# Nyström attention and a feed-forward layer on one core: batches 1 to 7 move to batch 0's tile layout, and the DMA crossbar turns q and k

## The chip, the cores and the metric

The kernel runs on one core of a Trainium2 chip, in one launch. The metric is device time in microseconds. The kernel before takes 267.89 us in the median of three runs (267.88, 267.89, 268.66).

## The reference

Eight batches, eight heads, 576 tokens, head size 64; 32 landmarks, each the mean of 18 consecutive tokens. Cut to what is computed:

```
q_lm, k_lm = means of q and k over segments of 18 tokens      # 32 landmarks
A = softmax(q k_lm^T / 8);  Bm = softmax(q_lm k_lm^T / 8);  C = softmax(q_lm k^T / 8)
Z = Bm^T / (norm1(Bm) * norminf(Bm))
six times:  Z = 2 Z - Z Bm Z
x   = A Z C v                     # heads side by side: (8, 576, 512)
xn  = (x - mean(x)) / sqrt(var(x) + 1e-6) * g_ln
out = x + relu(xn W1) W2          # W1: 512 x 2048, W2: 2048 x 512
```

Inputs and output are fp32; the kernel computes its products in fp16 with fp32 sums.

## The kernel before

**Units and stages.** A unit is four heads of one batch, so a batch has two units (u = 0, 1). For each unit q, k and v are loaded as 576 KB tiles `stg` (128 partitions: a head pair times 64 token groups; nine tokens in the row of each), cast to fp16 (`nat` for q and k, `natv` for v), q and k are turned so that the head dimension lies on the partitions (`xT`), and landmark sums are formed. Then follow the k scores, the exponentials, their product with v (`pscv`), the iteration on 32x32 blocks (`st`), the q scores (`ea`), and their divisors (`psd`, `lns`). The attention is not written out and read again: the 32x64 heads matrix Z C v is turned (`pszt`, `zt`), multiplied into W1 (`bank<-w,zt` or `psm`, copied to `m`), and the first layer takes `m` and `ea` directly (`psh`, then ReLU into `hT`). The rows of x themselves (`xblk`) are formed once, for the mean, the variance and the residual (`bank<-zcbd,ea`, `six`, `stats`, `rstd`). The second layer is `bank<-w,hT`; batches 4 to 7 do 512 of their 576 rows with seven half-size products in place of eight (`w2mix`).

**Batch 0** (`attention0`) is turned by TensorE against an identity (`pst`), each 128x128 block at once. Its landmark sums are nine 128x64 matmuls against `pm16`; q's landmarks are masked per head into `qbd`, so that `psc` multiplies full 128-row columns of `xT` by `qbd`, 18 matmuls a unit, and the result is exponentiated straight into the layout that `pscv` needs (`ect`). The q scores `psa` take 64-row pieces.

**Batches 1 to 7** (`Coming`, `attention2`, in the sets (1), (2), (3, 4), (5, 6), (7)) are turned by VectorE as 32x32 blocks of fp16 pairs seen as uint32 (`StreamTranspose xT<-nat`). That leaves rows of 32 partitions, so the scores are 32x32 tiles of TensorE with 288 columns, in two accumulated halves (`psec`, `psea`); the k scores are exponentiated by three ScalarE steps a unit (`ec`) and turned once more by VectorE (`ecT`). Landmark sums come in three ways: nine 128x128 matmuls against `pairs16` and a small turn (`tot`, `lmt`; batch 1 and half of set (3, 4)), VectorE sums over `xT` (`part<-xT`), or four adds on GpSimd (`asum`, `s`); `spread16` then distributes them (two matmuls a pair of units, `lm`).

**W1** holds g_ln and has its column means taken off so that the layer norm's mean drops out. `less(f)` is the mean of a quarter of W1. Up to batch `LAST_WHOLE` = 1 the copies of `m` add that term (`SCALAR_TENSOR_TENSOR m<-less,zsum,bank`); after it `center_w1` subtracts it from W1 itself in eight VectorE steps (`w<-w,less`), and `m` is a plain copy on whichever of ScalarE and VectorE is free sooner (`sooner`).

**What sets the order.** The program is written at build time by a planner. `Clock` keeps an estimated time for each engine and tile. Five streams (0 attentions, 1 totals, 2 first layers, 3 rows of batch 0, 4 second layers) yield when their next step can start, and the first stream in that list that can go now does:

```
            at = [when(k) for k in range(len(streams))]
            k = next((k for k in range(5) if at[k] <= now), None)
```

Between steps `help_out` issues stores, loads, casts, VectorE jobs, measuring and centring when the clock says that the engine is about free. The table `AFTER` holds a given step back until another stream has come so far (33 entries before). All engines run their own instructions strictly in the order written. All loads and stores but a few at the end go through SyncE's queue; SBUF buffers are rings (`stage` 6, `nat` 6, `xT` 4 for q and 4 for k), and PSUM has two two-bank tiles (`ps2`) and four single banks.

The helper `keep` (line 248) records every instruction; so most rows of the profile have line 298 (VectorE, ScalarE, GpSimd), 304 (`MM`), 308 (`TR`), 313, 321 and 323 (loads; the latter two load the second unit of v in three pieces, `load_swapped`), 434 and 451 (W1 and W2) or 1216 (stores), and are told apart by their tiles.

Of the kernel before, what the change touches and what calls it, by code (L numbers as in the profile page):

```python
# [20 lines left out]
def kernel(  # L21
# [63 lines left out]
    class Clock:  # L85


        WAY = 55.0
        OVERLAP = {"Activation": 110, "DVE": 80, "Pool": 30}
# [41 lines left out]
        def took(self, i, e, n, m):  # L131
            op = type(i).__name__
            if e == "Activation":
                return 300 if n < 8 else 190 + (1.07 if name_of(i.outs[0].bass_ap).startswith("ec_") else 0.79) * n
# [22 lines left out]
        def note(self, i):  # L157
# [33 lines left out]
            elif e == "PE":  # L191
                cols = count[0]
                if self.count == self.mark - self.LEAD:
                    self.ahead = self.now()
                if self.count == self.mark:
                    self.mark += self.BLOCK
                    ready = max(ready, self.fetched)
                    asked = max(self.ahead, self.fetched - 200)
                    behind = max([w for t, w in self.loads if t <= asked] + [0.0])
                    self.fetched = max(asked + 1200, behind + 400) + 2450  # L200
                self.count += 1
                rows_, cols_ = tuple(i.tile_size)
                self.cells.append((self.now(), cols / 2.4 * rows_ * cols_ / 128 ** 2))
                if tuple(i.tile_size) == (128, 128):
                    if self.small:
                        self.free[e] = max(list(self.lanes.values()) + [self.free[e]]) + 100
                        self.small, self.lanes = False, {}
                    start = max(self.free[e], ready)
                    self.free[e] = start + max(cols / (1.2 if start < 5200 else 2.4) + 3, 56)
                    done = self.free[e] + 160  # L210
                else:
                    if not self.small:
                        self.small, self.lanes = True, {}
                        self.free[e] += 95
                    elif self.shape != (rows_, cols_):
                        self.free[e] = max(list(self.lanes.values()) + [self.free[e]]) + 85
                    self.shape = rows_, cols_
                    lane = [(a, c) for a in range(i.tile_position[0], i.tile_position[0] + rows_, 32)
                            for c in range(i.tile_position[1], i.tile_position[1] + cols_, 32)]
                    start = max([self.free[e], ready] + [self.lanes.get(x, 0.0) for x in lane])  # L220
                    self.lanes.update((x, start + max(cols / 2.4, 30)) for x in lane)
                    self.free[e] = start + (8 if rows_ == 64 and cols < 128 else 4)
                    done = self.lanes[lane[0]] + 160
            else:
                start = max(self.free[e], ready)
                self.ready = start
                done = start + self.took(i, e, count[0], max(count[1:] + [0]))
                self.free[e] = done - self.OVERLAP[e]
                if e == "Pool":
                    self.pool = self.pool[-8:] + [(start, done)]  # L230
                if e == 'DVE' and count[0] == 1024 and writes[0] in parted_w1:
                    self.free['Pool'] = max(self.free['Pool'], start) + 430
            for n in reads:
# [69 lines left out]
    def MM(o, l, r, rb=0, cb=0, start=True, stop=True, skip=False):  # L303
        keep(nc.tensor.matmul(o, l, r, start=start, stop=stop, tile_position=(rb, cb),  # L304
                              skip_group_check=(skip or cb != 0)))

    def TR(o, i_, idn):
        keep(nc.tensor.matmul(o, i_, idn, is_transpose=True, tile_position=(0, 0)))


    def load(src, b, u, queue, t=None):
# [4 lines left out]
        return t  # L316

    def load_swapped(src, b, u, queue):
        t = stage.tile([P, 2, NJ, D], FP32, name="stg", tag="stg")
        heads = src[b, 4 * u:4 * u + 4].rearrange("h (t j) d -> h t j d", j=NJ)  # L320
        keep(queue.dma_start(out=t[:, 0, :, :], in_=heads[1:3].rearrange("h t j d -> (h t) j d")))
        for e in range(2):
            keep(queue.dma_start(out=t[ts(1 - e, 64), 1, :, :], in_=heads[3 * e]))
# [10 lines left out]
    for u in range(U):  # L334
# [19 lines left out]
    pairs16 = const.tile([P, 2, 2, LM], FP16, name="pairs16")  # L354
    nc.gpsimd.tensor_copy(
        out=pairs16[:], in_=pm16[:].rearrange("p (e l) -> p e l", e=2)[:, :, None, :]
        .broadcast_to([P, 2, 2, LM]))

# [12 lines left out]

    heads4 = const.tile([P, 2, 2, 2], FP32, name="heads4")
    for x in range(2):
        for e in range(2):
            nc.gpsimd.tensor_copy(out=heads4[:, x, :, e], in_=mask4[:, ts(e ^ x, 2)])
    heads_of = [heads4[:, x, :, :].rearrange("p r e -> p (r e)") for x in range(2)]
    spread16 = const.tile([P, 2, 2, 2, LM], FP16, name="spread16")
    nc.gpsimd.memset(spread16[:], 0.0)
    for half in range(2):
        for e in range(2):  # L380
            sl = ds(64 * e + 32 * half, 32)
            nc.gpsimd.tensor_copy(
                out=spread16[sl, half, e, :, :],
                in_=ident16[sl, sl][:, None, :].broadcast_to([LM, 2, LM]))
# [174 lines left out]

    heads, ready, multiplied, cast_v = {}, set(), {0}, {0}  # L560
# [8 lines left out]
    def attention0():  # L569
# [5 lines left out]
        def p2(shape, dtype, name):  # L575
            return ps2.tile(shape, dtype, name=name, tag="p2")

        qbd = asm.tile([P, W * 2, 2, LM], FP16, name="qbd", tag="qbd", bufs=1)
        dve.tensor_tensor(
            out=qbd[:],  # L580
            in0=nat_pss[0][:].rearrange("p u (e l) -> p (u e) l", e=2)[:, :, None, :]
            .broadcast_to([P, W * 2, 2, LM]),
            in1=mask2[:, None, :, None].broadcast_to([P, W * 2, 2, LM]), op=ALU.mult)
        yield "q's landmarks"
        klm = asm.tile([P, W, 64], FP16, name="klm", tag="klm", bufs=1)
# [6 lines left out]
        for w in range(W):  # L592
            for h in range(4):
                e, r = h // 2 ^ w, h % 2
                MM(psb[ds(32 * h, 32), w, :], qbd[ds(64 * r, 64), 2 * w + e, r, :],
                   klm[ds(64 * r, 64), w, ds(32 * e, 32)], rb=64 * r, cb=32 * h)
# [5 lines left out]
        for w in range(W):  # L602
            psc = p2([P, NJ, 64], FP32, "psc")
            for j in range(NJ):
                for e in range(2):
                    MM(psc[ds(64 * e, 64), j, :], early_xT["k", w][:, j, ds(64 * e, 64)],
                       qbd[:, 2 * w + e, :, :], cb=64 * e)
            t = aexp.tile([P, NJ, 64], FP16, name="ect", tag="e")
            act(t[:], psc[:], AF.Exp, scale=sc_C)
            ect.append(t)  # L610
# [17 lines left out]
        def scores_of_q(w):  # L628
            psa = p2([P, NJ, 64], FP32, "psa")
            for (j0, j1) in ((0, 8), (8, NJ)):  # L630
                for h in range(4):
                    r, e = divmod(h, 2)
                    rows, cb = ds(64 * r, 64), 32 * (2 * (e ^ w) + r)
                    MM(psa[ds(cb, 32), j0:j1, :], klm[rows, w, ds(32 * e, 32)],
                       early_xT["q", w][rows, j0:j1, ds(64 * e, 64)], rb=64 * r, cb=cb)
            t = aexp.tile([P, NJ * 64], FP16, name="ea", tag="e")
            act(t[:], psa[:].rearrange("p j t -> p (j t)"), AF.Exp, scale=sc_A)
            ea.append(t[:])

        warm(4, 256)  # L640
# [4 lines left out]

        def cv_of(w, h, half=None):
            at, n = ((D + 1) * (h % 2), D) if half is None else ((D + 1) * (h % 2) + 32 * half, 32)
            return cv[ds(32 * h, 32), w, ds(at, n)]
# [26 lines left out]
        zt = asm.tile([P, 2, W, LM], FP16, name="zt", tag="zt")  # L675
        for w in range(W):
            pszt = p2([P, 2, 512], FP32, "pszt")
            for h in range(4):
                e, r = h // 2 ^ w, h % 2
                sl = ds(32 * h, 32)  # L680
                for half in range(2):
                    cb = 64 * e + 32 * half
                    MM(pszt[ds(cb, 32), r, 0:LM], cv_of(w, h, half), st[sl, w, LM:],
                       rb=32 * h, cb=cb)
            scalar.copy(zt[:, :, w, :], pszt[:, :, 0:LM])
# [3 lines left out]
        for w in range(W):  # L689
            for h in range(4):  # L690
                sl = ds(32 * h, 32)
                MM(pszc[sl, w, :], st[sl, w, LM:], cv_of(w, h), rb=32 * h, cb=32 * h)
# [83 lines left out]
    class Coming:  # L776
        def __init__(self, bs, by_dve, by_pe=()):
# [7 lines left out]
            self.jobs = []  # L785
            for i, (nm, w) in enumerate(self.parts[:2 * n]):
                self.jobs.append((self.turn, i))
# [1010 lines left out]
```

## Time and profile before

| | before |
|---|---|
| median of three runs | 267.89 us (267.88 to 268.66) |
| span of the profiled execution | 266.1 us |
| the profiled execution's own time | not recorded apart; the median is 1.8 us above the span |
| granted TensorE clock, mean | 0.999 |
| instructions | 8332 |
| DMA | 46.68 MB, of it 36.70 MB read from HBM and 9.44 MB written |

The page gives busy time by engine, then forty slices of 6.65 us each in tenths, DMA queues, the chain of waits that ended last, and the costliest groups. A matmul's duration in a row includes its way through the array; matmuls overlap, so the distance between starts is less than the duration (a 128x512 `bank<-w,hT` has 380 ns in its row). "Idle before" is the engine's idle time ahead of the group, with what ended it.

### The profile page before, as it was taken

To read this page: it belongs to the slowest core of one execution; us is meant where nothing else is said; L and a number is where in the kernel's file an instruction comes from. 1 tells how busy PE (TensorE), PEld (TensorE's weight loads), DVE (VectorE), ACT (ScalarE), POOL (GpSimd) and SP (SyncE) were. 2 spreads that over 40 slices of the span, in tenths; PEclk is the share of its full clock that TensorE was granted. 3 is DMA by queue.
4 is the path that set the end of the run, shared out by engine and by line. 5 is a ranking of instruction groups with operands and counts; after the bars stand their busy time and mean duration, and the time that the engine had idled before them with its cause. 6 is when DMAs were issued, how large, how long until landed. Compare 5 with 4: busy or idle time off the path is not lost.

```text
span 266.1 us, 8332 instructions
## 1 busy us (share of the span) xinstructions
PE 256.5 (96%) x3442; PEld 167.9 (63%) x3442; DVE 202.8 (76%) x461; ACT 175.2 (66%) x337; POOL 133.6 (50%) x160
## 2 busy tenths in 40 slices
PE   7889998999999999999999999999999999999994
PEld 7644754466545554546655465578878765788883
DVE  2657873899999979788984986989684599819762
ACT  2578997378868896589797559787377654871000
POOL 5288788999729387499999934500000042000000
PEclk9999999999999999999999999999999999999999
DMA  7999999999976996766611120110060006100606
GB/s 253 380 396 389 388 386 393 317 343 306 354 237 172 388 363 187 207 174 198 200 43 39 34 52 2 42 43 0 2 158 0 2 4 160 43 0 2 158 17 183
DMA packets 23566, 46.68 MB, mean 175 GB/s; under 512 B 2404, under 2 KB 2664, under 8 KB 23528
## 3 DMA queue, kind: packets, MB, share of 16 engines
q1 hardware_dynamic: 23048, 45.49, 53.3%
q10 hardware_dynamic: 480, 0.66, 0.7%
q8 instruction: 27, 0.44, 0.7%
q14 instruction: 11, 0.09, 0.1%
HBM read 36.70 MB, written 9.44 MB: 173 GB/s over the span
## 4 chain that ended last, share of the span: by engine, by line
PE 78%; DMA 11%; DVE 3%; POOL 3%; issue 2%; SPq 1%; ACT 1%; POOLq 0%; DVEq 0%
PE bank L304 51%; PE psh L304 21%; DMA stg<-in_v_dram 6%; DMA wstg<-in_moe_w_ch_dram 3%; DMA stg<-in_q_dram 2%; PE pscv L304 1%; POOL natv L298 1%; PE psd L304 1%; DVE xblk L298 1%; PE psec L304 1%; PE psm L304 1%; PE psea L304 1%; POOL w L298 1%; SPq L313 1%; DVE st L298 1%
## 5 line engine op out<-in xcount | busy, mean ns | idle before, releaser
L304 PE MATMUL bank<-w,hT 128*128 128x512 f16 (+3 forms) x528 | 111.7, 335 | 1.2 <-issue 0.8
L298 ACT ACTIVATE hT<-psh 128x576 f16<-128x576 f32 x119 | 73.6, 654 | 21.9 <-PE psh L304 21.0
L304 PEld LDWEIGHTS <-hT 128*128 128x128 f16 x656 | 60.3, 98 | 32.5 <-issue 8.6
L304 PE MATMUL psh<-ea,m 128*128 128x288 f16 x512 | 78.3, 286 | 0.6 <-DVE ea L298 0.3
L304 PEld LDWEIGHTS <-m 128*128 128x128 f16 x512 | 48.8, 97 | 20.2 <-issue 3.7
L298 DVE SCALAR_TENSOR_TENSOR xblk<-bank,rstd,xblk 128x256 f32<-128x256 f32 (+2 forms) x77 | 39.0, 539 | 22.4 <-PE bank L304 22.3
L298 POOL TENSOR_TENSOR ea<-ea,lns 128x576 f16<-128x576 f16 x14 | 18.9, 1371 | 60.4 <-ACT lns L298 54.6
L298 POOL CAST nat<-stg 128x1152 f16<-128x1152 f32 x21 | 23.8, 1147 | 8.5 <-DVE xT L298 6.4
L298 DVE BATCH_NORM_STATS2 six<-xblk 128x6 f32<-128x512 f32 x36 | 24.2, 673 | 0.9 <-ACT xblk L298 0.9
L298 POOL CAST natv<-stg 128x1152 f16<-128x1152 f32 (+1 forms) x17 | 19.3, 1165 | 9.7 <-DMA stg<-in_v_dram 7.7
L298 DVE STREAM_TRANSPOSE xT<-nat 128x576 uint32<-128x576 uint32 x28 | 21.4, 763 | 0.0
L298 ACT COPY xblk<-bank 128x512 f32<-128x512 f32 (+1 forms) x32 | 18.0, 591 | 4.0 <-PE bank L304 3.7
L304 PE MATMUL bank<-w2mix 128*128 128x256 f16 x128 | 17.1, 273 | 0.0
L304 PE MATMUL bank<-w2mix,hT 128*128 128x256 f16 x128 | 15.8, 273 | 0.0
L298 DVE SCALAR_TENSOR_TENSOR st<-st,bank 128x128 f16<-128x128 f16 (+2 forms) x36 | 11.1, 308 | 5.9 <-PE bank L304 5.7
L298 ACT CAST m<-bank 128x512 f16<-128x512 f32 x18 | 9.9, 586 | 7.5 <-PE bank L304 7.4
L298 DVE TENSOR_REDUCE part<-xT 128x32 f16<-128x576 f16 x20 | 14.6, 744 | 0.2
L298 ACT ACTIVATE lns<-psd 128x576 f32<-128x576 f32 x16 | 10.3, 644 | 6.0 <-PE psd L304 5.9
L304 PE MATMUL bank<-zcbd,ea 128*128 128x256 f16 x80 | 14.1, 273 | 0.0
L298 DVE SCALAR_TENSOR_TENSOR m<-less,zsum,bank 128x512 f16<-128x512 f16 (+1 forms) x18 | 11.5, 682 | 3.0 <-PE bank L304 1.4
L304 PEld LDWEIGHTS <-w2mix 128*128 128x128 f16 x128 | 12.4, 98 | 2.0 <-issue 0.2
L304 PEld LDWEIGHTS <-st 32*32 32x32 f16 x448 | 5.9, 90 | 11.9 <-DVE st L298 8.9
(135 smaller groups left out, 365.9 us busy)
## 6 DMA issues: line engine op xcount, KB each, us to landing
stg<-in_q_dram SPq DMA_DIRECT2D x16, 576.0 KB, 6.3
stg<-in_k_dram SPq DMA_DIRECT2D x16, 576.0 KB, 6.0
out_dram<-xblk SPq DMA_DIRECT2D x66, 128.0 KB, 2.4
wstg<-in_moe_w_ch_dram SPq DMA_DIRECT2D x16, 512.0 KB, 7.3
stg<-in_v_dram SPq DMA_DIRECT2D x10, 576.0 KB, 7.2
stg<-in_v_dram SPq DMA_DIRECT2D x6, 288.0 KB, 6.2
stg<-in_v_dram SPq DMA_DIRECT2D x12, 144.0 KB, 6.0
out_dram<-xblk ACTq DMA_DIRECT2D x4, 128.0 KB, 3.2
```

Source lines behind the costliest of these rows:

```text
L298: return lambda *args, **kw: keep(getattr(self.engine, op)(*args, **kw))
L304: keep(nc.tensor.matmul(o, l, r, start=start, stop=stop, tile_position=(rb, cb), skip_group_check=(skip or cb != 0)))
L313: keep(queue.dma_start(out=t[:], in_=src[b, 4 * u:4 * u + 4].rearrange("(r e) (t j) d -> (e t) r j d", e=2, j=NJ)))
```

## The change

- Sets (1) to (7) use batch 0's layout: `nat` is [128, 9, 128], `xT` is a full turn [128, 9, 128], and k scores, exponentials, products and q scores are the same code for all batches (`scores_of_landmarks`, `scores_k`, `scores_q`, `masked_q`, `heads_to_rows`).
- q and k of batches 2 to 7 are turned by a DMA transpose on SyncE's queue, SBUF to SBUF, 24 in all; those of batch 1 by TensorE, as batch 0's. VectorE turns none.
- Landmark sums: batch 1 by TensorE (`pm16`, nine matmuls a tile); k of batches 2 to 7 by one VectorE sum over `xT`; q of batches 2 to 7 by GpSimd's four adds and one 128x64 matmul.
- `pairs16`, `spread16`, `lm`, `lmt`, `ec`, `ecT` and `load_swapped` go; v of all units is one load and one cast.
- `LAST_WHOLE` is 0: W1 is centred after batch 0's products, and batch 1's `m` are plain copies.
- The planner prices a DMA transpose (`TURN_ISSUE`, `TURN_WIRE`), takes a second-layer step in place of a first-layer step when an attention step is due within 400 ns (`SOON`), lets second-layer steps wait for W2's casts, and has a new `AFTER` table of 15 entries. `attention0` has four more filler matmuls.

The diff, cut to its core:

```diff
+        TURN_ISSUE, TURN_WIRE = 700.0, 1000.0
...
+            elif type(i).__name__ == "InstDmaTransposeAnt":
+                start = max(self.free[e], ready)
+                self.free[e] = start + self.TURN_ISSUE
+                self.wire = max(start + 1650, self.wire) + self.TURN_WIRE
+                self.loads = self.loads[-24:] + [(start, self.wire)]
+                done = start = self.wire + 600
...
+    def masked_q(lm):
+        t = asm.tile([P, 2 * U, 2, LM], FP16, name="qbd", tag="qbd", bufs=3)
+        dve.tensor_tensor(out=t[:], in0=lm..., in1=mask2x..., op=ALU.mult)
+        return t
+
+    def scores_k(x, qbd, xT):
+        psc = ps2.tile([P, NJ, 64], FP32, name="psc", tag="p2")
+        for j in range(NJ):
+            for e in range(2):
+                MM(psc[ds(64 * e, 64), j, :], xT[:, j, ds(64 * e, 64)],
+                   qbd[:, 2 * x + e, :, :].rearrange("p r l -> p (r l)"), cb=64 * e)
+        t = aexp.tile([P, NJ, 64], FP16, name="ect", tag="e")
+        act(t[:], psc[:], AF.Exp, scale=sc_C)
+        return t
+
+    def scores_q(pair, klm, xT):
+        tiles = {x: ps2.tile([P, NJ, 64], FP32, name="psa", tag="p2") for x in pair}
+        for (j0, j1) in ((0, 8), (8, NJ)):
+            for e in range(2):
+                for r in range(2):
+                    for x in pair:
+                        rows, cb = ds(64 * r, 64), 32 * (2 * (e ^ x) + (r ^ x))
+                        MM(tiles[x][ds(cb, 32), j0:j1, :], klm[rows, x, ds(32 * e, 32)],
+                           xT[x][rows, j0:j1, ds(64 * e, 64)], rb=64 * r, cb=cb, skip=True)
...
         def turn(self, i):
             nm, w = self.parts[i]
-            t = aprep.pin(aprep.tile([P, 2, NJ, LM, 2], FP16, name="xT", tag="xT" + nm, bufs=4))
-            n16 = self.n16[i]
-            dve.transpose(t[:].rearrange("p r j t x -> p (r j t x)").bitcast(UINT32),
-                          n16[:].rearrange("p r j d -> p (r j d)").bitcast(UINT32))
+            t = aprep.pin(aprep.tile([P, NJ, P], FP16, name="xT", tag="xT" + nm, bufs=4))
+            keep(nc.sync.dma_start_transpose(
+                out=t[:], in_=self.n16[i][:].rearrange("p j r d -> p (j r d)")))
             self.used(i)
...
+        def add_up(self, i):
+            ...
+                dve.tensor_reduce(
+                    out=self.lm[nm, w // 2][:, w % 2, :],
+                    in_=self.xT[nm, w][:].rearrange("p j (g a) -> p g j a", a=2),
+                    axis=AX.XY, op=ALU.add)
...
-    LAST_WHOLE = 1
+    LAST_WHOLE = 0
...
-    sets = [Coming((1,), (), ("k0", "k1", "q0", "q1"))]
+    sets = [Coming((1,), (), ("k0", "q0"))]
+    sets += [Coming(bs, [f"k{y}" for y in range(len(bs))]) for bs in ((2,), (3, 4), (5, 6), (7,))]
...
+                if c.turns:
+                    if c.turn_ready() <= now and clock.free["SP"] <= now + 500:
+                        c.next_turn()
...
+            if k == 2 and at[0] <= now + SOON and at[4] <= now:
+                k = 4
```

In the changed program TensorE has 3211 matmuls in place of 3442; VectorE 326 instructions in place of 383, ScalarE 175 in place of 210, GpSimd 112 in place of 104. SyncE's queue holds 24 transposes more and 12 split v loads less.

More of the change, by code (lines that the diff above doesn't have):

```diff
@@ L190, in note @@
                 start = done
[L191 to L223, printed above, removed]
@@ L592, in attention0 @@
         for w in range(W):
[L593 to L596, printed above, removed]
+            scores_of_landmarks(psb, w, qbd, klm, w)
         act(psb[:], psb[:], AF.Exp, scale=sc_B)
@@ L602, in attention0 @@
         for w in range(W):
[L603 to L610, printed above, removed]
+            ect.append(scores_k(w, qbd, early_xT["k", w]))
         cinv, _ = gram_of(p1([P, 4, W * LM], "psse"), st, bmT, W, lambda: warm(2, 256))
@@ L628, in scores_of_q @@
         def scores_of_q(w):
[L629 to L638, printed above, removed]
+            ea.extend(scores_q((w,), klm, {w: early_xT["q", w]}))
+        warm(4, 256)
         warm(4, 256)
@@ L833, in used, with turn_ready, job_ready @@
                 nat.unpin(self.n16.pop(i))
[L835 removed]
+        def turn_ready(self):
+            i = self.turns[0]
             if i not in self.n16:
                 return NEVER
[L838 to L842 removed]
+            return max(clock.at(self.n16[i]), aprep.next("xT" + self.parts[i][0]))
+        def job_ready(self):
+            i = self.jobs[0]
+            return clock.at(self.xT[self.parts[i]]) if self.parts[i] in self.xT else NEVER
@@ new lines, in lm_next, with add_ready, add @@
+        def lm_next(self, i):
+            nm, w = self.parts[i]
+            return asm.next("klm" if nm == "k" else "qbd")
+        def add_ready(self, i):
+            of = self.sums if self.how(i) == "pool" else self.n16
+            if i not in of or i + 1 not in of:
+                return NEVER
+            return max(clock.at(of[i], of[i + 1]), banks.next(), self.lm_next(i))
+        def add(self, i):
+            psl = banks.take([P, U, 64])
+            for x in range(U):
+                if self.how(i) == "pool":
+                    s16 = self.sums.pop(i + x)
+                    asm.unpin(s16)
+                    MM(psl[:, x, :], s16[:].rearrange("p r d -> p (r d)"), pm16[:], skip=True)
+                else:
+                    for j in range(NJ):
+                        MM(psl[:, x, :], self.n16[i + x][:, j, :, :].rearrange("p r d -> p (r d)"),
+                           pm16[:], start=(j == 0), stop=(j == NJ - 1), skip=True)
+                    self.used(i + x)
+            nm, w = self.parts[i]
+            if nm == "q":
+                t = masked_q(psl)
+            else:
+                t = asm.tile([P, U, 64], FP16, name="klm", tag="klm", bufs=3)
+                sooner(U * 64, clock.at(psl))(t[:], psl)
+            self.lm[nm, w // 2] = asm.pin(t)
@@ L843, in total, with pe_ready, turn_by_pe @@
+        def pe_ready(self, i):
+            nm, w = self.parts[i]
+            if i not in self.n16:
+                return NEVER
+            return max(clock.at(self.n16[i]), aprep.next("xT" + nm), ps2.next("p2"))
+        def turn_by_pe(self, i):
+            nm, w = self.parts[i]
+            n16 = self.n16[i]
+            pst = ps2.tile([P, NJ, P], FP16, name="pst", tag="p2")
             for j in range(NJ):
-                MM(psl, pairs16[:].rearrange("p e h l -> p (e h l)"), self.n16[i][:, :, j, :],
-                   start=(j == 0), stop=(j == NJ - 1))
```

438 lines of the change are left out of this document (180 added, 258 removed), and 12 rows, old and new, of the table AFTER.

## The prediction

> **What bounds the kernel now.** The first view is the page's busy shares, then its forty slices.
>
> ```profile
> PE 256.5 (96%) x3442; PEld 167.9 (63%) x3442; DVE 202.8 (76%) x461; ACT 175.2 (66%) x337; POOL 133.6 (50%) x160
> PE   7889998999999999999999999999999999999994
> DMA  7999999999976996766611120110060006100606
> PE 78%; DMA 11%; DVE 3%; POOL 3%; issue 2%; SPq 1%; ACT 1%; POOLq 0%; DVEq 0%
> ```
>
> TensorE is busy in every slice after the first three, and 78% of the chain that ended last is TensorE. The 11% DMA lies in the first 38 us, where inputs and weights stream in. So after about 46 us the time is a sum over TensorE instructions; before that it is set by arrivals. The stretches show where the other engines are close behind:
>
> ```profile
> 40.00:50.00 10.00, 9.16 (x171) 4.13 (x170) 5.15 (x17) 4.77 (x9) 9.31 (x9) 1.00 1.05 391
> 50.00:66.00 16.00, 16.00 (x127) 10.01 (x126) 15.74 (x30) 12.35 (x21) 15.29 (x18) 1.00 1.02 311
> 82.00:100.00 18.00, 18.00 (x228) 11.26 (x227) 15.31 (x34) 16.63 (x34) 12.72 (x15) 1.00 0.97 338
> 120.00:140.00 20.00, 19.87 (x158) 12.16 (x156) 17.77 (x37) 17.92 (x34) 19.37 (x22) 1.00 0.48 146
> ```
>
> (Columns: stretch, its length, busy us of TensorE, weight loads, VectorE, ScalarE, GpSimd, granted clock, DMA share, GB/s.) At 40 to 50 us TensorE lacks 0.84 us and VectorE has half its time free; at 50 to 66 us VectorE is full; at 120 to 140 us GpSimd nearly is. The granted clock is 1.00 in each stretch, so it does not enter.
>
> The profiled span is 266.1 us. The profiled execution's own time outside the span is not given; the median of three runs, 267.89, lies 1.8 above the span, and I carry those 1.8 unchanged. About 0.3%, 0.8 us, is what a measurement of this kernel can tell from no change.
>
> **TensorE's sum.** What one step costs in the stream is the distance from start to start, read from merged timeline rows: a row of n instructions lasts (n-1) steps and one full duration.
>
> ```profile
> 10.54 0.44 PE L304 MATMUL bank<-pm,nat 128*128 128x64 f16 x9 [0.23 <-DVE nat L298]
> 10.81 0.67 PE L308 MATMUL pst<-ident,nat 128*128 128x128 f16 x9
> 12.25 0.76 PE L304 MATMUL psc<-qbd,xT 128*64 128x64 f16 x36
> 14.54 0.42 PE L304 MATMUL psa<-xT,klm 64*32 64x512 f16 x8
> 29.62 0.68 PE L304 MATMUL bank<-nat,pairs 128*128 128x128 f16 x9
> 34.45 0.72 PE L304 MATMUL psec<-xT,lmt 32*32 32x288 f16 x32
> ```
>
> - Landmark totals by `pairs16`: 72 leave, (0.68-0.22)/8 = 57 ns each: -4.1 us.
> - `spread16`: 10 of 256 columns leave. Three 256-column fillers take 0.49 us with 0.27 for the last, so 108 ns each: -1.1.
> - k scores: for each of seven pairs of units, `psec` (0.72) becomes `psc` (0.76): +0.3.
> - q scores: `psea` takes 0.57 a pair (3.98 us over seven). The new `psa` takes 0.42 for one unit alone, which fills half of the array's cells, so a pair lies between 0.42 and 0.85. I take 0.47: the W1 products also fill all cells with eight 512-column steps and take 0.41, and eight 64-column steps follow. -0.7, bounds -1.0 and +2.0.
> - Batch 1 turned by TensorE: 36 transposes at (0.67-0.22)/8 = 56 ns, +2.0, and 36 sums through `pm16` at (0.44-0.19)/8 = 31 ns, +1.1. Twelve sums of the pre-added tiles: +0.4.
> - Landmark scores (16 small matmuls to 4 a pair) and the turn of zt (16 to 8): about -0.5. `pscv` keeps its count and shape: 0.
>
> The sum is -2.6 us: +1.0 in batch 1 and -3.6 in batches 2 to 7. The two parts meet different limits.
>
> **Batch 1, 20 to 46 us.** In the changed order q's two transposes and their sums stand ahead of chunk 7 of batch 0's first layer. They wait for the fourth `nat` cast, which ends at 31.5 us (starts 30.34, takes 1.15). Walking the new order with the old durations puts TensorE some 3 us behind at 32.6 us. But the last W2 cast ends at 45.1 us (44.08 plus 1.04), second-layer matmuls wait for it, and the old order had run out of other work there: of its gaps over 100 ns, 0.62 us at 40.2, 0.24 at 42.5 and 0.46 at 43.9, and a filler. W2's last loads stay where they were in the queue. Walking on, the new order reaches batch 1's zt turn at about 48.2 us against 46.3, with eight more second-layer matmuls done, worth 1.75 us. That is level: 0 on the path; if that cover fails, up to +3.
>
> **W1 centred a batch sooner.** Eight VectorE steps of 0.76 (5.8 us) leave the full stretch at 50 to 66 us and go to about 23 to 42 us, where VectorE has idle time. Batch 1 may not begin its first layer until all are done; `rstd` and the softmax of batch 1 queue behind them on VectorE. Eight fused `m` copies of 0.74 become plain casts of 0.59 on ScalarE or 0.68 on VectorE. I count 0; up to +1 if the centring delays batch 1's softmax.
>
> **Off the path.** VectorE loses
>
> ```profile
> L298 DVE STREAM_TRANSPOSE xT<-nat 128x576 uint32<-128x576 uint32 x28 | 21.4, 763 | 0.0
> L298 DVE TENSOR_REDUCE part<-xT 128x32 f16<-128x576 f16 x20 | 14.6, 744 | 0.2
> L298 DVE STREAM_TRANSPOSE ecT<-ec 128x320 uint32<-128x320 uint32 x14 | 6.8, 494 | 5.9 <-ACT ec L298 5.9
> ```
>
> and some 12 us of smaller steps, and gains 12 k sums of 1152 elements (1.3 us each, from 744 ns for 576: 15.9), seven masked q tiles of 0.42 and some 7 us of copies: about -30 us. ScalarE loses 42 `ec` steps (15.7), `lm`, `tot` and four casts (9.6), and gains 14 `ect` of 0.65 and some 5 us: about -12. GpSimd gains four casts of 1.15 and two chains of pre-adding of 2.87, less one half-tile `natv` cast: about +9. Idle engines save nothing by themselves. Waits over 100 ns on TensorE after 66 us sum to only 2.9 us; I take none of it and keep it for the range.
>
> **The DMA transposes.** Twenty-four of 288 KB each, on SyncE's queue among loads and stores. No row shows one. Nearest rows:
>
> ```profile
> stg<-in_k_dram SPq DMA_DIRECT2D x16, 576.0 KB, 6.0
> out_dram<-xblk SPq DMA_DIRECT2D x66, 128.0 KB, 2.4
> stg<-in_v_dram SPq DMA_DIRECT2D x12, 144.0 KB, 6.0
> L304 PE MATMUL psec<-xT,lm x160: 282/283/298, 66.9 to 209.5; 32*32 32x288 f16 x160
> ```
>
> Lower bound, as plain bytes at 390 GB/s: 0.76 us of all DMA engines, 18 us in total; the whole-tile v loads give some back. Upper bound, if each holds the path for a whole landing as in the third row: 6 us. Need: batch 2's casts run from 48 us; its k scores start at 66.9 (last row's first start), those of batches 3 and 4 at 96.2 and 99.2. Twelve tiles in 48 us is 4 us each; the other sets leave 4.5 and more. Under 4 us they are hidden behind TensorE's matmuls, at no cost. I take 1 to 2 us, since moving contiguous rows in 288 KB is nearest to the plain loads. GpSimd's cast stands ahead of each, and behind it on SyncE's queue wait the next loads and stores, whose own slack is tens of us after 80 us.
>
> On this the Trainium skill speaks twice. "VectorE: DVE Perf Modes", section on the three transpose paths, gives 1309 ns for one 128x128 tile by the crossbar; nine in a row would be an estimated 11.8 us a tile and the kernel would end near 390 us. "Advanced Engine Details and Errata", section on X-Bar Transpose (TRN2), says these are as fast as regular DMAs, at 350 to 400 GB/s; the forecast then stands as it is. No run here shows either yet.
>
> **Forecast.** -3.6 + 0 + 0: 266.1 - 3.6 + 1.8 = 264.3, which I give as 264.4 from the median. Its own range, by the q-score bounds and the gaps, is 263 to 266.5.
>
> **Rivals.**
> - *Late landing blocks the in-order queues (slower).* Each k sum sits in VectorE's queue and each k-score step in TensorE's, placed where the planner expects the tile: 1.65 + 1.0 + 0.6 = 3.25 us after issue when the wires are idle. Loads land in 6 to 7 us while DMA is full. With 2.5 us of lateness at the three pairs whose turn falls before 110 us, on the k and half as much on the q side, 3 x 3.75 = 11 us less 3.6: 275; with 1 us each, 268.5. I take 271. It turns the sign when the six pairs lose over 0.6 us each. For it: VectorE is nearly full at 50 to 66. Against: the planner counts queued transfers, and each set had 20 us. Chance 0.22.
> - *The crossbar is paid block by block (much slower).* At 6 us each, twelve tiles last until 120 us against 98: +22, near 287. It decides from 4 us. Chance 0.08.
> - *The early stage is not level.* The 3 us behind at 32.6 us is not made up: 267.5, no change. Chance 0.10.
> - *Relief counts.* VectorE's 30 and ScalarE's 12 us end the 2.9 us of waits: 261.5. Chance 0.13. That the change would not do what it says I set aside: the program issues 24 DMA transposes and no VectorE transpose of q or k.
>
> **How the numbers follow.** The forecast has 0.47. The third rival's 0.10 lies on both sides of no change, as 0.02, 0.05 and 0.03. Faster: 0.47 + 0.13 + 0.02 = 0.62; same: 0.05; slower: 0.22 + 0.08 + 0.03 = 0.33. The range 260.5 to 273 leaves out the block-by-block crossbar, the late tail of the first rival and a little below.
>
> **What would show it.** Right: 3211 TensorE matmuls, the granted clock at 1.00, `psa` pairs near 0.47 us, transposes landing well under 4 us apart, `psh` of batch 2 starting some 1 us sooner and the gain growing to 3.6 by 210 us; VectorE near 173 us busy. Wrong: gaps on TensorE ahead of `psc` or `psa`, VectorE idle before the `klm` sums with a DMA named as releaser, or batch 1's first `psh` later than 50 us.

## The result and the profile after

The changed kernel takes 282.91 us (median; 281.03 to 284.41) against 267.89: a ratio of 1.0545, 95% interval 1.0495 to 1.0595. It is slower by 15 us. The forecast was 264.4 with a range that ended at 273. The profiled execution has a span of 280.4 us. All ratios in this document leave out runs that are over 1.5% longer than the shortest of the same kernel: one of four in e2, two in e11, and three each in e7 and e8, which are therefore given without a ratio and whose profiles are of such runs.

First the page of the changed kernel: busy shares, slices of 7.0 us, shares of the chain.

```profile
PE 259.8 (93%) x3211; PEld 169.3 (60%) x3211; DVE 182.3 (65%) x395; ACT 166.9 (60%) x296; POOL 142.4 (51%) x177
PE   7899899988789897499999999999999999999994
PEclk9999999999979999599999999999999999999999
DMA  7999999899999999999998611120033003500606
PE 53%; POOL 16%; DMA 14%; issue 6%; DVE 4%; ACT 3%; SPq 1%; POOLq 0%; ACTq 0%
```

TensorE has the 3211 matmuls of the forecast, but now there are holes in the slices from 56 to 119 us (mostly 7 and 8, and one of 4), TensorE's share of the chain has gone from 78% to 53%, and what came in is GpSimd (16%) and DMA. The DMA row stays at 8 or 9 until 154 us; before, slices of 6 and 7 began at 73 us. The slices after 120 us are as full as before. The same in stretches (columns as in the prediction):

```profile
50.00:66.00 16.00, 14.90 (x119) 7.92 (x113) 11.60 (x22) 9.39 (x18) 14.24 (x17) 1.00 0.96 211
66.00:82.00 16.00, 12.39 (x174) 6.84 (x166) 7.33 (x16) 7.54 (x15) 8.89 (x11) 0.90 1.13 288
100.00:120.00 20.00, 14.51 (x206) 7.80 (x207) 6.61 (x14) 10.29 (x17) 12.28 (x14) 0.83 1.10 319
```

At 66 to 82 and at 100 to 120 us no engine is full: TensorE lacks 3.6 and 5.5 us and VectorE is idle more than half the time, while the DMA engines are over full (the share adds up the packets' times, which overlap where it is over 1). The two large holes in TensorE's timeline (start, duration, idle time before and what ended it) and what VectorE did in the second:

```profile
73.56 1.69 PE L331 MATMUL bank<-w,hT 128*128 128x512 f16 x7
78.16 0.24 PE L331 MATMUL bank<-st 32*32 32x64 f16 x8 [2.92 <-DVE st L325]
78.70 2.13 PE L331 MATMUL bank<-w,hT 128*128 128x512 f16 x5
...
116.00 0.40 PE L331 MATMUL bank<-st 32*32 32x64 f16 x16 [5.49 <-DVE st L325]
116.94 2.31 PE L331 MATMUL bank<-w,hT 128*128 128x512 f16 x5
```

```profile
107.49 0.31 DVE L325 STREAM_TRANSPOSE bmT<-st 128x128 f16<-128x128 f16 x1
113.19 1.35 DVE L325 TENSOR_REDUCE klm<-xT 128x64 f16<-128x1152 f16 x1 [5.40 <-DMA xT<-nat]
...
115.65 0.29 DVE L325 TENSOR_TENSOR st<-bank,cinv 128x128 f16<-128x128 f32 x1
```

TensorE waits for `st`, the next step of set (3, 4)'s iteration. TensorE's product for it ran at 108.0 us, but in its queue a k sum of batch 5 stands ahead, and that waits 5.40 us for a DMA transpose that lands at 113.2. So the late tile of the next set stops the present set, by way of an in-order queue. All twelve k sums together waited 16.9 us. What the transposes themselves did (first line: the source line's instructions with shortest, median and longest time on SyncE in ns; second: from issue to landing; then SyncE's timeline):

```profile
L956 SPq DMA_TRANSPOSE xT<-nat x24: 1272/1892/4046, 54.1 to 154.4; - x24
DMA to landing us min/median/max: 3.2/5.4/8.5
```

```profile
67.67 3.52 SPq L956 DMA_TRANSPOSE xT<-nat  x1
71.27 1.19 SPq L1153 DMA_DIRECT2D out_dram<-xblk  x2
72.57 5.50 SPq L956 DMA_TRANSPOSE xT<-nat  x2
78.12 1.09 SPq L342 DMA_DIRECT2D stg<-in_q_dram  x2
```

A load or store holds SyncE about 0.55 us. A transpose holds it 1.27 to 4.05 us, 47.8 us over all 24 (the planner's `TURN_ISSUE` is 0.7), and the q loads of batch 4 behind them are issued at 78.1. The last load of all is issued at 142.4 us, before at 125.6.

One more measure is used below. The distance from the start of a matmul to the start of the next is either streaming (216 ns for 512 columns, 56 for 128, as long rows show) or time beyond it, called lost here. Before, TensorE streamed 233.9 us and lost 26.9; after, it streams 231.9 and loses 43.1. The streaming fell by 2.0, and 16.2 us more are lost, 15 of them between 60 and 130 us.

### The profile page after: what moved, and what is told of

The parts are those of the page before. It is cut to its first block, busy times and chain, and to the rows that moved or that the text cites. A ratio compares the mean times of both kernels' runs of the same rounds, so it can differ in the third digit from the quotient of the medians.

```text
span 280.4 us, 7785 instructions
## 1 busy us (share of the span) xinstructions
PE 259.8 (93%) x3211; PEld 169.3 (60%) x3211; DVE 182.3 (65%) x395; ACT 166.9 (60%) x296; POOL 142.4 (51%) x177
## 3 DMA queue, kind: packets, MB, share of 16 engines
q1 hardware_dynamic: 51272, 52.57, 67.2%
## 4 chain that ended last, share of the span: by engine, by line
PE 53%; POOL 16%; DMA 14%; issue 6%; DVE 4%; ACT 3%; SPq 1%; POOLq 0%; ACTq 0%
PE bank L331 34%; PE psh L331 14%; DMA xT<-nat 7%; DMA stg<-in_k_dram 7%; POOL asum L325 6%; POOL nat L325 4%; POOL ea L325 3%; POOL natv L325 2%; PE pscv L331 2%; DVE klm L325 1%; PE psd L331 1%; ACT xT L325 1%; POOL s L325 1%; DVE ea L325 1%; PE psa L331 1%
## 5 line engine op out<-in xcount | busy, mean ns | idle before, releaser
L325 ACT ACTIVATE hT<-psh 128x576 f16<-128x576 f32 x117 | 72.4, 652 | 18.0 <-PE psh L331 17.0
L325 POOL TENSOR_TENSOR ea<-ea,lns 128x576 f16<-128x576 f16 x14 | 17.8, 1285 | 48.7 <-ACT lns L325 47.0
L325 POOL CAST nat<-stg 128x1152 f16<-128x1152 f32 x25 | 28.6, 1153 | 8.5 <-DMA stg<-in_k_dram 5.6
L325 DVE TENSOR_REDUCE klm<-xT 128x64 f16<-128x1152 f16 x12 | 16.2, 1348 | 16.9 <-DMA xT<-nat 16.9
L325 POOL CAST natv<-stg 128x1152 f16<-128x1152 f32 x16 | 18.3, 1168 | 11.1 <-DMA stg<-in_v_dram 10.1
L325 ACT CAST m<-bank 128x512 f16<-128x512 f32 x22 | 12.3, 586 | 12.4 <-PE bank L331 12.1
L325 ACT ACTIVATE ea<-psa 128x576 f16<-128x576 f32 x16 | 9.6, 647 | 15.4 <-PE psa L331 15.4
L331 PE MATMUL bank<-st 32*32 32x64 f16 (+1 forms) x384 | 9.4, 194 | 9.1 <-DVE st L325 8.9
L331 PE MATMUL bank<-w2mix,hT 128*128 128x256 f16 x128 | 15.9, 273 | 0.0
L325 POOL COPY hT<-hT 128x1024 f16<-128x1024 f16 x4 | 4.1, 1037 | 21.8 <-ACT lnv L325 18.2
L325 POOL TENSOR_TENSOR asum<-asum 128x256 f32<-128x256 f32 (+1 forms) x24 | 14.1, 589 | 1.9
```

Of the source, the lines that this page charges most:

```text
L325: return lambda *args, **kw: keep(getattr(self.engine, op)(*args, **kw))
L331: tc.keep_in_program_order(nc.tensor.matmul(o, l, r, start=start, stop=stop, tile_position=(rb, cb), skip_group_check=(skip or cb != 0)))
```

## Experiments

Letters for theories change between groups: D and S belong to e1 to e4, P and X to e9, and A, B and C to the others. The median of the kernel before, measured anew beside each group of experiments, lay between 267.2 and 268.4, so differences between groups are uncertain by about 1 us.

**The order's prices (e1, e2, e11).** If the sums merely stand too early in the queues, a planner that is told of later tiles puts them later.

```diff
 e1:  -done = start = self.wire + 600        # a transpose's landing
      +done = start = self.wire + 3600
 e2:  -TURN_ISSUE, TURN_WIRE = 700.0, 1000.0
      +TURN_ISSUE, TURN_WIRE = 1900.0, 1000.0
 e11: +TURN_ISSUE, TURN_WIRE = 1900.0, 2000.0, and self.wire + 1600
```

> The same instructions as the changed kernel, but the planner is told that a DMA transpose lands 3 us later (3600 in place of 600 after its wire time), so it places the k sums and the k scores later in the queues. Theory D (the k sums stand in VectorE's queue ahead of their tiles and hold what is behind them): VectorE's 16.9 us of waits for xT fall under 5 us and the time falls to 268 to 272 us. Theory S (SyncE's queue and the DMA paths cannot deliver the tiles in time, whatever the order): 278 us or more, with the same waits elsewhere.

> The planner is told that a DMA transpose occupies SyncE's queue for 1.9 us, the median of the profile after, in place of 0.7. Theory D: partly mended, 270 to 277 us. Theory S: the order of loads and transposes on SyncE's queue changes little, 278 to 284 us.

> The changed kernel with the planner told what the trace shows of a DMA transpose: 1.9 us to issue (0.7 in the changed kernel), 2.0 us of all DMA engines (1.0) and 1.6 us to land after that (0.6); the order follows from it. If the loss is one of order (steps placed before their tiles can be there), most comes back: 268 to 273. If the DMA engines simply have no room for the transposes while loads and stores fill them, the waits move to other steps and it stays at 277 to 284.

Measured: e1 282.70 (ratio 1.054, 1.0465 to 1.0615), e2 284.18 (1.0582, 1.0529 to 1.0634), e11 281.67 (276.67 to 284.02; 1.0386, 1.0297 to 1.0476). In e1 VectorE's wait for `klm` halved, from 16.9 to 7.8 us, and TensorE still lost 42.5: it waited in other places, 2.2 us for GpSimd's `s` until 78.5 us and 2.7 us for VectorE's `cv` until 118.6. Placement alone is not the cause; it decides only where the wait is seen. At most 4 to 5 us came back, in e11 (1.0386 x 268.17 is 278.5).

**Other ways to sum or turn (e3, e4, e10).**

```diff
 e3:  k's sums of batches 2 to 7 by nine pm16 matmuls over nat, none by VectorE
 e4:  -self.turns = list(range(2 * n)) if not by_pe else []
      +self.turns = [i for i in range(2 * n) if self.parts[i][0] == 'k'] if not by_pe else []
      # q of batches 2 to 7: batch 0's turned tile is read in its place
 e10: -sets += [Coming(bs, [f"k{y}" ...]) ...]
      +sets += [Coming(bs, (), [f"k{y}" ...], True) ...]   # q, k turned by TensorE, k summed there
```

> k's landmark sums of batches 2 to 7 come from the cast tile by nine TensorE matmuls (12 x 0.28 = 3.4 us more on TensorE), so no VectorE instruction reads a transposed tile; the DMA transposes stay. Theory D: no VectorE wait for xT is left and the time is 267 to 273 us. Theory S: TensorE waits for xT itself before psc, 277 us or more.

> q of batches 2 to 7 is not turned: its scores read batch 0's turned q tiles. 12 transposes in place of 24, all else the same. Theory S: with half of SyncE's transposes gone the queue keeps up, 264 to 268 us. Theory D: the k sums still stand too early behind the first tiles; 270 to 276 us.

> The changed kernel with q and k of batches 2 to 7 turned by TensorE as batch 1's are (36 transposes a batch, copies of the turned tiles by ScalarE or VectorE), k's sums by pm16 on TensorE, q's by GpSimd; no DMA transpose; the planner puts it in an order of its own. TensorE's sum grows by 6 x 36 x 56 ns = 12.1 us of turns and 6 x 18 x 31 ns = 3.3 us of sums, so about 282 with stalls like those of before. If the crossbar costs 13 us in the changed kernel, this one is level with it, 279 to 286, and its stalls on TensorE stay under 33 us (43.1 in the changed kernel). If something else in the feed is late, the stalls stay above 38 and the time is above 290.

Measured: e3 293.72 (1.0957, 1.0917 to 1.0997). VectorE's queue no longer waits for the crossbar, and TensorE loses more (50.9). The time is that of S, but TensorE waits for other things than S had it: for the casts themselves (`nat`), for GpSimd's sums of q (`s`) and for ScalarE's copies of `m` (total in us, times, longest):

```profile
PE bank L331 <- POOL nat L325: 5.0, 3, 2.4
PE psh L331 <- ACT m L325: 3.6, 2, 3.3
PE bank L331 <- POOL s L325: 3.6, 1, 3.6
```

The whole feed is late, casts too. e4 277.74 (1.0357, 1.0311 to 1.0404): twelve transposes fewer give back 5 us, less than either theory had. e10 285.73 (1.0651, 1.0624 to 1.0678): 15 us more streaming (247.0), as worked out, and only 31.9 lost. With no crossbar most of the lateness is gone.

**The same order, other transfers (e5, e6, e9).** The three above change the planner's order with the price. Here each instruction of TensorE, VectorE, ScalarE and GpSimd stands where the changed kernel has it, and SyncE's too; only the 24 transfers differ. The planner goes on pricing them as transposes.

```diff
-keep(nc.sync.dma_start_transpose(out=t[:], in_=nat "p j r d -> p (j r d)"))
 e5: +keep(nc.sync.dma_start(out=t[:, 0, :], in_=nat[:, 0]), "turn")            # 32 KB
 e6: +keep(nc.sync.dma_start(out=t "p (j t)", in_=nat "p (j r d)"), "turn")     # 288 KB, rows of 2304 bytes
 e9: +keep(nc.sync.dma_start(out=t[:, :, 0:P], in_=nat), "turn")                # 288 KB, all xT tiles with 16 spare columns
```

> The changed kernel with every instruction in the same order on every engine, except that each of the 24 DMA transposes is a plain copy of one ninth of the tile (128 x 256 bytes, 32 KB, SyncE's queue, same waits and same waiters); the sums and scores of batches 2 to 7 read that ninth nine times, so the values differ and the work does not. Theory A (issuing a transpose holds SyncE for 1.3 to 4 us and the loads behind it are late) and theory B (the transposes' 256-byte packets fill the DMA engines and all landings are late) both expect the order to hold as it was written: 264 to 268 us, VectorE's waits for klm under 4 us, last load issued before 130 us. Theory C (the rest of the change, GpSimd's sums and the order itself, starves the scores) expects 277 to 283.

> As the changed kernel in the same order, but each DMA transpose is a plain copy of the whole tile (same 288 KB, rows of 2304 bytes, untransposed, so the values differ). A: a plain issue takes about 0.55 us, so the loads are early again: 265 to 269. B by bytes alone: as the changed kernel, 276 to 283; B by packets (2304-byte rows in place of 256-byte packets): between, 266 to 272. C: 277 to 283.

> The changed kernel in the same order, but each DMA transpose is a plain, untransposed copy of the whole tile (the values differ) into a tile with 16 spare columns in each of its nine rows, so that it must go in 1152 packets of 256 bytes, as the transpose does, and not in rows of 2304 bytes. Theory P (the size of the packets is what makes a transpose dear: 27.7 ns for 256 bytes, 2.0 us of all engines a tile): as the changed kernel, 277 to 284, landings 4 to 8 us. Theory X (the crossbar path itself is dear, in its issue and in what it does to the loads beside it): as with whole rows, 268 to 272, each packet well under 20 ns.

| 24 transfers, same order | us | ratio, 95% interval | time on SyncE's queue, us | DMA engines (queue share x span), us | TensorE lost, us | last load issued, us |
|---|---|---|---|---|---|---|
| a ninth, plain (e5) | 267.46 | 0.9987, 0.9969 to 1.0006 | 12.1 | 146.2 | 28.8 | 129.1 |
| whole, rows of 2304 bytes (e6) | 269.58 | 1.0053, 1.0030 to 1.0077 | 12.1 | 159.0 | 30.0 | 130.2 |
| whole, packets of 256 bytes (e9) | 277.01 | 1.0329, 1.0286 to 1.0372 | 19.7 | 173.0 | 37.7 | 137.7 |
| crossbar (the changed kernel) | 282.91 | 1.0545, 1.0495 to 1.0595 | 47.8 | 188.4 | 43.1 | 142.4 |

(55.0% of 265.9, 59.5% of 267.2, 62.9% of 275.0 and 67.2% of 280.4 us give the fifth column.) The first two lines settle C: the rest of the change does not starve anything. The lines of the copies in e6 and in e9, and of the k sums in e5:

```profile
L956 SPq DMA_DIRECT2D xT<-nat x24: 465/495/562, 53.8 to 140.6; - x24
```

```profile
L956 SPq DMA_DIRECT2D xT<-nat x24: 594/650/2738, 54.2 to 148.2; - x24
```

```profile
L325 DVE TENSOR_REDUCE klm<-xT 128x64 f16<-128x1152 f16 x12 | 16.0, 1333 | 0.9 <-DMA xT<-nat 0.9
```

Moving 288 KB instead of a ninth costs 2.1 us; cutting it into 256-byte packets 7.4 more; the crossbar itself 5.9 more. P said that the packets do it all, X that the crossbar does: both do, about half each. A packet of 256 bytes took 19.0 ns on average in e9, as X set it, and 27.7 in the changed kernel. In e9 the other instructions of SyncE were held too (45.7 us between 50 and 145 us, 32.9 in e6; why is not shown), so queue and engines still rise together.

**Holding the queue alone (e13, e14).** e6 with empty instructions behind each copy, no traffic added:

```diff
 keep(nc.sync.dma_start(out=t ..., in_=nat ...), "turn")          # as e6
+for _ in range(30):                                              # e14: 60
+    tc.keep_in_program_order(nc.sync.drain())
```

> The run with plain copies of the whole tile (e6: 269.6 us, 12 us of issue in all on SyncE for the 24 copies), same order, and behind each copy 30 empty instructions on SyncE's queue that only hold it, no extra traffic. I put one at 30 to 60 ns, so 0.9 to 1.8 us a copy; the trace will say. Theory A (time in which SyncE is held is what costs): from e6, e9 and the changed kernel SyncE's held time and the loss go together at about 0.37 us for each us held, so 24 copies by 1.2 us is +29 us held, +10 us, about 280. Theory B (packets on the DMA engines cost, the held queue is only their echo): 269 to 272.

> The same with 60 empty instructions behind each copy, 1.8 to 3.6 us a copy. A: beyond the changed kernel, 285 to 300. B: little until the queue itself is late by several us; 271 to 280, below the changed kernel although SyncE is held longer than there.

An empty instruction took 61 to 67 ns of the queue on average, so a copy held SyncE for 2.54 us (60.9 in all) and 4.17 (100.0). Measured: 282.74 (1.058, 1.0524 to 1.0636) and 311.40 (1.162, 1.1552 to 1.1687). e13 has the changed kernel's time and its picture, holes in the same places with the same releasers, though packets and bytes are those of e6:

```profile
79.67 0.24 PE L331 MATMUL bank<-st 32*32 32x64 f16 x8 [3.15 <-DVE st L325]
...
115.16 0.40 PE L331 MATMUL bank<-st 32*32 32x64 f16 x16 [5.00 <-DVE st L325]
```

```profile
112.36 1.35 DVE L325 TENSOR_REDUCE klm<-xT 128x64 f16<-128x1152 f16 x1 [4.91 <-DMA xT<-nat]
```

So A holds: time on SyncE's queue is enough to make this loss. In the changed kernel it need not be all of it, since e13 holds the queue longer for the same time. e6 to e13 is 13.2 us for 48.8 us held, 0.27 each, and e13 to e14 0.73 each, beyond A's range, so the price rises. The crossbar holds the queue 35.7 us longer than e6, at 0.27 worth 9.6 of the 13.3 us that it costs; by this estimate some 4 us are left for the DMA engines. Counting everything that holds SyncE from 50 us on, its loads and stores too, gives 68.3 us in e6, 90.1 in e9, 103.8 in the changed kernel and 111.2 in e13. The price is then 0.31, and the queue alone would account for 10.9 of the 13.3 us, and for 6.7 of e9's 7.4. So the queue is the larger part by either estimate, and what the DMA engines cost by themselves is not measured.

**Relieving the queue (e7, e8, e15).** The transposes stay, and part of SyncE's work is issued by ScalarE, in the same order.

```diff
 e7:  +load(..., nc.scalar if b > 2 else queue)     # loads of batches 3 to 7
 e8:  +keep(nc.scalar.dma_start_transpose(...), "turn")
 e15: +keep(nc.scalar.dma_start(out=to, in_=half), "store")   # stores that SyncE had
```

> The changed kernel in the same order, with the loads of batches 3 to 7 issued on ScalarE's queue in place of SyncE's, so that no load stands behind a transpose. A: the loads come as early as the order has them, some 0.5 us of ScalarE each; the transposes themselves are still issued late only by one another: 268 to 273, and batch 5's first load is issued before 92 us (96.9 before). B and C: 279 to 285, as the landings or the sums are what is late.

> The changed kernel in the same order, with the 24 transposes issued on ScalarE's queue in place of SyncE's. A: SyncE's loads are early, but ScalarE is held 1.3 to 2.5 us at each transpose, 24 x 1.9 = 45 us over 100 us, so exponentials and ReLUs come late: 272 to 290, with the stalls on TensorE now ended by ScalarE. If the issue on ScalarE measures 1.3 us each and never more, then what stretched it on SyncE was the loads queued in the same ring. B: loads no earlier than in the changed kernel, transposes landing as late as before, 280 to 290.

> The changed kernel, DMA transposes and all, in the same order, with the stores that SyncE issued (about 0.55 us each, some 22 of them between 50 and 145 us) issued on ScalarE's queue. Theory A (SyncE's held time costs, 0.3 to 0.4 us for each us): SyncE is relieved of some 12 us in that stretch, so 278 to 280, and the last load is issued 3 to 5 us sooner than at 142.4. Rival: what ScalarE's queue helped nothing with for the loads it does not help with here, since stores on another queue mix into the transposes on the DMA engines and ScalarE is held by them: 283 to 292, transposes' landing median above 6.5 us (5.4 in the changed kernel).

Measured: e7 298.85 (291.57 to 302.09), e8 315.79 (306.30 to 320.14), e15 287.13 (1.0715, 1.0669 to 1.0760). All three missed: e7 and e8 are beyond every theory, e15 has its rival's time but not by the transposes. In e7 the transposes held SyncE longer than in the changed kernel (61.9 us in all, one of them 8.0) and landed later (median 6.9, longest 16.3 us), and batch 5's first load came at 95.2, hardly sooner than 96.9. In e8 single transposes held ScalarE up to 10.0 us. In e15 the transposes behaved as in the changed kernel (48.6 us, median landing 5.4), the last load came only 1.3 us sooner, and ScalarE spent 39.5 us on issuing (3.8 in the changed kernel), so that TensorE waited for its `hT`. In none of the three did a second queue help. Why the transposes take longer beside another queue's loads is left open; B's part, the engines' time, is the natural candidate (a 256-byte packet took 33.1 ns in e7) and was not separated.

**W1 centred sooner, alone (e12).**

```diff
-    LAST_WHOLE = 1
+    LAST_WHOLE = 0      # in the kernel before
```

> The kernel before with W1 centred after batch 0's products in place of batch 1's (LAST_WHOLE = 0) and nothing else changed. Forecast: no cost on the path, 267 to 269. Rival: batch 1's softmax and first layer come late and the old order table no longer fits, 269 to 273.

Measured: 279.51 (1.0418, 1.0381 to 1.0454), beyond the rival. One line of TensorE's timeline has two fifths of it:

```profile
41.65 1.01 PE L304 MATMUL bank<-w,hT 128*128 128x512 f16 x2 [4.76 <-POOL w L298]
```

With the old table TensorE reaches the last chunks of W2 before GpSimd has cast them: batch 1's first k scores, which lay ahead of them at 34.5 us, now come at 45.6. In the changed order it does not happen (from 40 to 50 us 2.2 us are lost, before 2.6); which part of the new order prevents it was not tried.

No version tried beats the kernel before; e5, whose transfers are nearly free, only equals it.

## Why the prediction was wrong

- **The step that failed: the DMA transposes, taken at 1 to 2 us each, "hidden behind TensorE's matmuls, at no cost".** They cost 15.4 us, from e5's 267.46 (which still moves a ninth of each tile) to 282.91. The time on the wire was about right: the 27,648 packets of 256 bytes took 27.7 ns each, which is 2.0 us of all 16 engines a tile. What had no price was the issue: SyncE is held 47.8 us where plain copies hold it 12.1. The words that went by it were "behind it on SyncE's queue wait the next loads and stores, whose own slack is tens of us after 80 us". They say nothing of the time before 80 us, in which eight of the transposes were issued, and after it the slack was not there either. Batch 4's q loads were issued at 78.1 us, in e5 at 70.4 and before at 62.9. Batch 5's first load shows the same (before, e5, after):

```profile
81.48 2.54 SPq L313 DMA_DIRECT2D stg<-in_k_dram  x2
87.72 1.10 SPq L342 DMA_DIRECT2D stg<-in_k_dram  x2
96.86 2.51 SPq L342 DMA_DIRECT2D stg<-in_k_dram  x2
```

  So 6.2 us of its delay are the new order's and 9.2 the transposes'. The test "under 4 us each" compared a rate with a need, and a queue is not a rate.
- **The mechanism of the first rival was right, its size was not.** It had k sums in VectorE's in-order queue, tiles late by 1 to 2.5 us at pairs due before 110 us, 271. It put the lateness on landings beside a full DMA; the runs put the larger part on the queue that issues. The waits were 2.5, 2.8, 2.0 and 5.4 us at 59, 76, 92 and 113 us. It let each wait count once; that a stop of TensorE also delays what frees the buffers of the next loads was left out. That this made the last wait the longest is argued; the rising price from e13 to e14 fits it. "Each set had 20 us", which spoke against it, was read from the old order's dates.
- **The Trainium skill's two rules.** By "VectorE: DVE Perf Modes" (three transpose paths) one 128x128 tile takes 1309 ns; nine in a row, 11.8 us, did not show: the quickest tile of nine blocks landed 3.2 us after its issue, and tiles issued in a run landed about 1 us apart. By "Advanced Engine Details and Errata" (X-Bar Transpose) they are as fast as regular DMAs. The section's figure of 350 to 400 GB/s is a little above the closest landings (294,912 bytes each 0.95 to 1.06 us are 278 to 310 GB/s), and it says nothing of the issue: in the same order and bytes the plain copies of e6 made the kernel 13.3 us faster.
- **The block-by-block rival** (287) is near in number and wrong in kind, by the same landings: its twelfth tile was to land at 120 us and landed at 102.7.
- **TensorE's sum was right**, -2.0 streamed against -2.6. `psa` takes 0.44 us a pair in six of its seven rows (0.47 forecast; 0.68 behind the second hole); `pst` of batch 1 goes at 56 ns and `pm16` at 29 (56 and 31).
- **The -3.6 did not reach the end all the same.** With the transfers nearly free (e5), 2.1 us less streaming meet 1.9 more lost, and the time is 267.46: the third rival's 267.5, which had 0.10. Two lines of e5's timeline show where:

```profile
30.95 0.66 PE L336 MATMUL pst<-ident,nat 128*128 128x128 f16 x9 [0.87 <-ACT xT L325]
...
61.12 0.65 PE L331 MATMUL psh<-ea,m 128*128 128x288 f16 x4 [0.74 <-ACT hT L325]
```

  Batch 1's turn by TensorE waits for the copy of the tile before (lost from 20 to 30 us: 2.65, before 1.40), and its first layer, which starts at 56.7 and not at 49.9 us, waits for its own ReLUs (60 to 70 us: 2.80, before 0.67). The step "That is level: 0 on the path" is where this belongs: batch 1's zt turn, walked to 48.2 us, came at 49.7, and the sign that was set for it, a first `psh` later than 50 us, came. That e5 lands on the third rival's number by this rival's mechanism, and that the delay to 56.7 makes the second wait, is argued, not shown.
- **W1 centred: 0** fits the changed order, where the eight steps end at 43.6 us and batch 1's first layer starts at 56.7; its price there was not measured alone. In the old order it cost 11.3 us (e12).
- **Off the path.** GpSimd 142.4 (forecast 143) and the k sums' 16.2 us (15.9) were right, VectorE's 182.3 was forecast as 173, ScalarE's 166.9 as 163. Nothing hung on it: relief did not count, as said.
- **Signs.** The count of matmuls came as set, and `psa` near it. The clock, VectorE's wait with a DMA as releaser and batch 1's late `psh` came on the wrong side, and `psh` of batch 2 starts at 88.3 us, not sooner than 82.4. The large gaps on TensorE stand ahead of the iteration's `st` products, not of `psc` or `psa`. The landings are split: about 1 us apart within a run, but the first twelve tiles took from 54.1 to 102.7 us, 4.0 us each, which is the limit that was set.

## What to carry to other kernels

A transfer that is new to a kernel has two prices: what it takes on the wire, and how long it holds the queue that issues it. The second is paid by all that stands behind, and where that queue feeds the engines it has to be bounded from the worst row, not set to nothing. To learn which part of a large change costs, keep the order of every engine and exchange only the suspected instruction for a cheaper one; a change of the planner's price also moves everything else. An order fitted by hand to one set of durations (the `AFTER` table) did not carry over even to a change of one constant (e12).

## What the runs showed of the hardware

- A DMA transpose of 288 KB from SBUF to SBUF held the issuing engine 1.27 us at least, 4.05 at most on SyncE, and up to 10.0 us on ScalarE with the loads on SyncE's queue (e8). The plain copy of the same tile held it 0.46 to 0.56 us.
- A plain copy in 256-byte packets in place of 2304-byte rows made the queue's packets 14.0 us dearer over 24 tiles (from 159.0 to 173.0 us of all engines), the crossbar another 15.4. A 256-byte packet took 19.0 ns in the plain copy and 27.7 through the crossbar; the 2304-byte rows stayed at 105 ns in all three kernels, so the loads beside them were not slowed packet by packet. The time rose by 7.4 us with the first step. The Trainium skill, "DMA: Bandwidth & Descriptors" (Why small descriptors are slow (HBM only)), has it that transfers within SBUF do not suffer the penalty of small descriptors; here, beside loads from HBM on the same engines, they took more time.
- After the idle stretches of 2.9 and 5.5 us the granted clock fell (0.90 and 0.83 over the stretches): five 512-column matmuls took 2.13 and 2.31 us. In e6, which has no such hole at 74 us, the same five took

```profile
75.00 1.25 PE L331 MATMUL bank<-w,hT 128*128 128x512 f16 x5
```

  The two rows together are 1.9 us longer than twice this, an echo of the holes. The Trainium skill, "TensorE: Matmul & The Clock Gate" (What's actually happening), has the clock halve after an idle window of about 3.4 us; the first hole was shorter, and the clock fell all the same.
